# Reordering the prologue of a fused adaLN, attention and SwiGLU kernel: score banks kept free, dummy matmuls, statistics and normalisations on other engines

## The chip, the cores and the metric

The kernel runs on one core of one Trainium2 chip. The metric is the device time of one execution in microseconds (us), lower is better. The kernel before takes 1299.07 us (median of 4 runs, 1298.13 to 1301.06).

Engines in the profile: PE is TensorE's matmuls and PEld its weight loads, DVE is VectorE, ACT is ScalarE, POOL is GpSimd, SP is the engine that issues the loads.

## The reference

One transformer block with modulation (adaLN): 2048 tokens, width 1024, 32 heads of 32 that share one K and one V head, a SwiGLU of width 3584. All inputs are bf16.

```python
mod = (silu(c) @ w_mod).reshape(1, 6, 1, -1)          # w_mod: 1024 x 6144
sa, ca, ga, sb, cb, gb = ...                           # its six parts
h = layernorm(x) * (1 + ca) + sa
q = h @ wq; k = h @ wk; v = h @ wv                     # 32 query heads, one K, one V
p = softmax(q @ k.T * 32 ** -0.5)
x = x + ga * ((p @ v) @ wo)
h = layernorm(x) * (1 + cb) + sb
x = x + gb * ((silu(h @ w1) * (h @ w3)) @ w2)
```

Only the prologue matters here: loading x and the modulation weights, the first layernorm, K, V and the first Q, until the exponentials of the scores flow on ScalarE.

## The kernel before

The kernel file contains its own list scheduler. Each instruction is a node with an engine, what it reads and writes, a priority and an *assumed* duration `dur`. `schedule()` plays the engines forward with these durations and fixes the order of the instructions on every engine; `emit()` writes each engine's stream in that order with semaphore waits. On the chip each engine then works through its stream in that order.

```python
G.add("pe", tr, reads=[("XN", q0 + i), "IDENT"] + xnk(q0 + i), dur=ncb * 0.065, ...)   # one node
...
    t_free[e] = s + d                     # schedule(): the engine is free after the assumed duration
...
# loads, in this order: x tiles 0-7, modulation weights, K, V, first slice of Q
xload(0, 8)
for k in range(NC):
    dma(... WM01[:, k, :], wmod_in[k * P:(k + 1) * P, 0:2 * D] ..., ("wm01", k), writes=[("UR", k)], ...)
dma(... WKV[:, 0], wk_in ...); dma(... WKV[:, 1], wv_in ...); dma(... WQ[:, :, 0:P] ...)
...
# modulation columns (128 matmuls of one column, in 8 packs, one for each load), then two copies on VectorE
for k in range(NC):
    G.add("pe", mm, reads=["SCT", ("UR", k)], dur=16 * 0.06, ...)
G.add("dve", ... MODC[:, 0, :] ...); G.add("dve", ... MODC[:, 1, :] ...)
...
def ln_norm(t, q):                        # (x - mean) * rstd, 128x1024, on VectorE
    G.add("dve", lambda e: e.tensor_scalar(xnt(q), X[:, s, :], MV[:, t, 0:1], RS[:, t:t + 1],
                                           ALU.subtract, ALU.mult), ..., dur=0.42, prio=2)
...
for tb in range(NTB):                     # four blocks of 512 tokens = 4 tiles each
    for i in range(4):
        ln_stats(tb * 4 + i)              # 2 statistics halves and an aggregate on VectorE
    ln_scale(tb * 4, 4)                   # rstd of 4 tiles, two small GpSimd instructions
    for i in range(4):
        ln_norm(tb * 4 + i, q0 + i)
    if tb + 2 < NTB:
        xl = xload(tb * 4 + 8, 4)
    ln_transpose(4, q0, ..., ("act", "dve") if tb < 2 else ("dve",))   # PE transposes, HREG evictions with MODC
    kv(tb)                                # K and V of this block
    if tb == 0:
        qproj(0, 0)
```

A step of attention needs the keys of two tiles; the first head group therefore takes 4 exponentials of 128x1024 from each block of tokens, and the 13th exponential is the first that needs the fourth block's keys. The eight PSUM banks are two general ones (PB) and six (SP) that become score banks with the first score.

Three words used below: an eviction is the copy of PE's results from a PSUM bank into a buffer; the HREG evictions write the normalised tokens, transposed and modulated, from which K, V and Q are projected; the modulation columns (MODC) are the scale and shift that these evictions apply. Row scales are the layernorm's rstd.

The softmax here doesn't subtract the row's maximum and nothing guards it: scores larger than these inputs give would overflow.

## Time and profile before

| | before |
|---|---|
| time, median | 1299.07 us |
| ScalarE busy | 1011.0 us, 78% of the span; 1024 exponentials are 969.6 us of it |
| modulation columns read by VectorE | 21.09 us |
| first exponential | 38.05 us |
| 13th exponential | 61.86 us |

The first part of the page (busy time of each engine, its share of the span, number of instructions):

```profile
span 1296.0 us, 26693 instructions
PE 1177.5 (91%) x11393; PEld 583.5 (45%) x11393; DVE 877.7 (68%) x1223; ACT 1011.0 (78%) x1174; POOL 20.8 (2%) x51
```

The timeline of ScalarE (start, duration, engine, line, operation, what is written from what, shapes, count, and in brackets the idle time before and what ended it). L509 are HREG evictions, L715 the exponentials:

```profile
21.36 2.79 ACT L509 ACTIVATE HREG<-SP,MODC 128x512 bf16<-128x512 bf16 x4 [18.93 <-DVE MODC L457]
...
38.05 1.94 ACT L715 ACTIVATE UREG<-SP 128x1024 bf16<-128x1024 f32 x2 [3.78 <-PE SP L704]
43.87 5.61 ACT L715 ACTIVATE UREG<-SP 128x1024 bf16<-128x1024 f32 x6 [3.88 <-PE SP L704]
51.62 3.77 ACT L715 ACTIVATE UREG<-SP 128x1024 bf16<-128x1024 f32 x4 [2.15 <-PE SP L704]
61.86 3.77 ACT L715 ACTIVATE UREG<-SP 128x1024 bf16<-128x1024 f32 x4 [6.47 <-PE SP L704]
66.23 22.36 ACT L715 ACTIVATE UREG<-SP 128x1024 bf16<-128x1024 f32 x24 [0.60 <-PE SP L704]
```

Read it as a count: 2 + 6 + 4 exponentials, then the 13th at 61.86 us. Before that ScalarE waits; after it the exponentials run almost without a gap. So the place where the prologue pays or loses is the 13th exponential.

What leads there, from the timelines of the other engines: the last pack of modulation matmuls (L450) waits for its load, the columns are read at 21.09 us, and the four K projections (L538, 8 matmuls each) follow.

```profile
20.47 0.58 PE L450 MATMUL PB<-SCT,UREG 128*128 128x1 bf16 x16 [0.92 <-DMA UREG<-in_w_mod_dram]
20.73 1.04 POOL L459 COPY WKR<-QT 128x1024 bf16<-128x1024 bf16 x1 [2.69 <-DMA QT<-in_A_wk_dram]
21.09 0.17 DVE L455 COPY MODC<-PB 128x8 f32<-128x8 f32 x1 [1.10 <-PE PB L450]
24.20 3.59 PE L538 MATMUL SP<-HREG,WKR 128*128 128x512 bf16 x8 [3.15 <-ACT HREG L509]
37.87 3.59 PE L538 MATMUL SP<-HREG,WKR 128*128 128x512 bf16 x8
47.56 1.90 PE L538 MATMUL PB<-HREG,WKR 128*128 128x512 bf16 x8 [0.38 <-DVE HREG L515]
58.66 1.90 PE L538 MATMUL PB<-HREG,WKR 128*128 128x512 bf16 x8 [2.32 <-DVE HREG L515]
```

The first two projections take 3.59 us and the last two 1.90 us for the same work: PE's clock is at half in the first two. The Trainium skill, "TensorE: Matmul & The Clock Gate" (Part 1), describes this: half the clock until about 3.4 us of sustained work. The trace agrees in the ratio (3.59 / 1.90 = 1.9). The granted clock in the profile reads 0.5 around the second projection (36.6 to 43.4 us) but 1.00 around the first (24.2 to 27.8 us), so for the first the half clock is read from the durations alone.

### The profile page before, as it was taken

To read this page: it belongs to the slowest core of one execution; us is meant where nothing else is said; L and a number is where in the kernel's file an instruction comes from. 1 tells how busy PE (TensorE), PEld (TensorE's weight loads), DVE (VectorE), ACT (ScalarE), POOL (GpSimd) and SP (SyncE) were. 2 spreads that over 40 slices of the span, in tenths; PEclk is the share of its full clock that TensorE was granted. 3 is DMA by queue.
4 is the path that set the end of the run, shared out by engine and by line. 5 is a ranking of instruction groups with operands and counts; after the bars stand their busy time and mean duration, and the time that the engine had idled before them with its cause. 6 is when DMAs were issued, how large, how long until landed. Compare 5 with 4: busy or idle time off the path is not lost.

```text
span 1296.0 us, 26693 instructions
## 1 busy us (share of the span) xinstructions
PE 1177.5 (91%) x11393; PEld 583.5 (45%) x11393; DVE 877.7 (68%) x1223; ACT 1011.0 (78%) x1174; POOL 20.8 (2%) x51
## 2 busy tenths in 40 slices
PE   5698998899898889868999999999999999999998
PEld 3343344554455555413333335545333336754477
DVE  7888867885457787746687777656887777633421
ACT  1499999999899999989999999989999996011100
POOL 1000000000000000000000000000000000000000
PEclk9898999999899999868999999999999999999999
DMA  9533001553456556500232344202433244255563
GB/s 313 195 103 112 2 2 50 148 155 107 114 133 176 144 151 181 145 1 2 66 89 84 90 121 112 62 1 67 130 98 94 83 109 115 60 174 150 161 173 90
DMA packets 239446, 141.31 MB, mean 109 GB/s; under 512 B 6880, under 2 KB 231136, under 8 KB 239328
## 3 DMA queue, kind: packets, MB, share of 16 engines
q1 hardware_dynamic: 239328, 139.61, 37.6%
q8 instruction: 90, 1.47, 0.5%
q14 instruction: 28, 0.23, 0.1%
HBM read 135.40 MB, written 4.19 MB: 108 GB/s over the span
## 4 chain that ended last, share of the span: by engine, by line
PE 43%; ACT 41%; issue 6%; DVE 6%; DMA 3%; SPq 1%; ACTq 0%; DVEq 0%
ACT UREG L715 38%; PE PB L809 9%; PE PB L838 7%; PE SP L704 5%; PE SP L809 5%; PE PB L659 5%; PE SP L838 5%; ACT HREG L818 3%; PE PB L786 2%; DMA WREG<-in_B_w_dram 1%; DVE UREG L744 1%; PE PB L554 1%; PE PB L760 1%; DMA WREG<-in_w_mod_dram 1%; DMA UREG<-in_w_mod_dram 1%
## 5 line engine op out<-in xcount | busy, mean ns | idle before, releaser
L715 ACT ACTIVATE UREG<-SP 128x1024 bf16<-128x1024 f32 x1024 | 969.6, 1172 | 60.6 <-PE PB L659 32.1
L809 PE MATMUL PB<-QT,WREG 128*128 128x512 bf16 (+1 forms) x1904 | 361.7, 331 | 6.8 <-DVE DSB L766 2.0
L749 DVE TENSOR_TENSOR UREG<-UREG 128x2048 bf16<-128x2048 bf16 x200 | 243.2, 1216 | 31.8 <-ACT UREG L715 29.2
L704 PE MATMUL SP<-QT,KT 32*128 32x512 bf16 (+1 forms) x2560 | 207.5, 348 | 57.8 <-ACT UREG L715 44.2
L809 PEld LDWEIGHTS PB<-QT,WREG 128*128 128x128 bf16 x1904 | 166.8, 98 | 160.7 <-issue 63.3
L744 DVE TENSOR_TENSOR UREG<-UREG 128x2048 bf16<-128x2048 bf16 x100 | 121.5, 1215 | 87.3 <-ACT UREG L715 86.7
L704 PEld LDWEIGHTS SP<-QT,KT 32*128 32x128 bf16 x2560 | 54.1, 92 | 245.4 <-ACT UREG L715 231.0
L838 PE MATMUL PB<-WREG,HREG 128*128 128x256 bf16 x1232 | 152.8, 273 | 2.7 <-DVE HREG L843 1.8
L659 PE MATMUL PB<-UREG,V 128*32 128x512 bf16 (+1 forms) x2528 | 138.1, 353 | 10.2 <-DVE HREG L820 4.6
L838 PEld LDWEIGHTS PB<-WREG,HREG 128*128 128x128 bf16 x1232 | 113.1, 98 | 40.3 <-issue 24.8
L818 ACT ACTIVATE HREG<-PB 128x512 bf16<-128x512 f32 (+1 forms) x126 | 82.2, 652 | 46.9 <-PE PB L809 42.7
L769 DVE RECIPROCAL DSB<-DSB 128x128 f32<-128x128 f32 x128 | 115.1, 927 | 0.5
L820 DVE SCALAR_TENSOR_TENSOR HREG<-HREG,PB 128x512 bf16<-128x512 bf16 (+1 forms) x126 | 71.0, 563 | 45.8 <-ACT HREG L818 37.7
L659 PEld LDWEIGHTS PB<-UREG,V 128*32 128x32 bf16 x2528 | 59.2, 99 | 69.9 <-issue 25.8
L818 ACT ACTIVATE HREG<-SP 128x512 bf16<-128x512 f32 x14 | 8.4, 597 | 94.5 <-PE SP L809 94.5
L809 PE MATMUL SP<-QT,WREG 128*128 128x512 bf16 x336 | 75.0, 379 | 0.0
L554 PE MATMUL PB<-HREG,WREG 128*128 128x512 bf16 x256 | 66.2, 384 | 1.2 <-DVE QT L557 1.1
L825 DVE TENSOR_TENSOR HREG<-HREG,PB 128x256 bf16<-128x256 bf16 (+1 forms) x112 | 60.8, 543 | 5.4 <-PE PB L809 3.9
L838 PE MATMUL SP<-WREG,HREG 128*128 128x256 bf16 x560 | 62.8, 273 | 1.3 <-DMA WREG<-in_B_w_dram 1.3
L838 PEld LDWEIGHTS SP<-WREG,HREG 128*128 128x128 bf16 x560 | 54.6, 98 | 8.8 <-DMA WREG<-in_B_w_dram 1.8
L786 PE MATMUL PB<-WO,QT 128*128 128x512 bf16 x208 | 54.7, 390 | 0.1
L809 PEld LDWEIGHTS SP<-QT,WREG 128*128 128x128 bf16 x336 | 32.9, 98 | 39.4
(88 smaller groups left out, 567.0 us busy)
## 6 DMA issues: line engine op xcount, KB each, us to landing
WREG<-in_B_w_dram SPq DMA_DIRECT2D x140, 512.0 KB, 4.1
WREG<-in_B_w_dram SPq DMA_DIRECT2D x20, 1792.0 KB, 8.2
X<-in_A_x_dram SPq DMA_DIRECT2D x32, 256.0 KB, 3.7
WREG<-in_w_mod_dram SPq DMA_DIRECT2D x16, 512.0 KB, 4.9
UREG<-in_w_mod_dram SPq DMA_DIRECT2D x8, 512.0 KB, 9.1
out_dram<-X SPq DMA_DIRECT2D x16, 256.0 KB, 3.4
WO<-in_A_wo_dram SPq DMA_DIRECT2D x1, 2048.0 KB, 16.0
WREG<-in_A_wq_dram SPq DMA_DIRECT2D x1, 1792.0 KB, 11.1
```

What stands on the lines that cost most here:

```text
L554: g = mm_group(NC, lambda e, b, c: e.matmul(b, WQ[:, c, f * P:(f + 1) * P], HT[:, c, sl], start=c == 0, stop=c == NC - 1), lambda c: [("WQ ...
L659: r = e.matmul(PB[g.bank][32 * gg:32 * gg + 32, 0:qn], V[:, kt, :] if kind == "V" else ONES[:], U[:, pu, (gg * npk + j) * qn:(gg * npk + j ...
L704: r = e.matmul(SP[:, b, o:o + w], KT[32 * gg:32 * gg + 32, kts[j] * P:(kts[j] + 1) * P], QT[32 * gg:32 * gg + 32, f, q0 + qo:q0 + qo + w], ...
L715: G.add("act", lambda e, u=u, h0=h0, n=n, b0=b0, nb=nb, wb=wb: e.activation(U[:, u, h0 * W:(h0 + n) * W].rearrange("p (b w) -> p b w", b=n ...
L744: G.add("dve", lambda e, tr=tr, u=u, fu=first_u: e.tensor_tensor(TR[:, tr, 0:4 * W], U[:, fu, 0:4 * W], U[:, u, 0:4 * W], ALU.add), reads= ...
L749: G.add("dve", lambda e, tr=tr, u=u: e.tensor_tensor(TR[:, tr, 0:4 * W], TR[:, tr, 0:4 * W], U[:, u, 0:4 * W], ALU.add), reads=[("TR", tr) ...
L769: G.add("dve", lambda e, h=h: e.reciprocal(DSB[:, h * 128:(h + 1) * 128], DSB[:, h * 128:(h + 1) * 128]), reads=["DSB"], writes=[("DSBr", ...
L786: g = mm_group(NC, lambda e, b, f, t=t, h=h: e.matmul(b, QT[:, f, t * P:(t + 1) * P], WO[:, f, h * 512:(h + 1) * 512], start=f == 0, stop= ...
L809: return e.matmul(b[:, o:o + qn], W13[sl][w][:, c, sub * P:(sub + 1) * P], QT[:, c, q0:q0 + qn], start=c == 0, stop=c == NC - 1)
L818: G.add("act", lambda e, g=g1: e.activation(TS[:, 0:qn], PB[g.bank][:, 0:qn], ACT.Tanh, scale=0.5), writes=["TS"] + alias("TS"), groups=[( ...
L820: G.add("dve", lambda e, g=g1: e.scalar_tensor_tensor(TT[:, 0:qn], TS[:, 0:qn], 1.0, PB[g.bank][:, 0:qn], ALU.add, ALU.mult), reads=["TS"] ...
L838: return e.matmul(b[:, j * 256:(j + 1) * 256], HHT[:, fc, (i0 + j) * P:(i0 + j + 1) * P], W2S[:, r, fc, :], start=fc == 0, stop=fc == NF - 1)
```

## The change

Its intent: get two blocks of tokens ready before the first score, let no other work take a score bank once scores flow, and so start the exponentials earlier and without interruption; keep PE's clock up with dummy matmuls during the first loads; take statistics and a quarter of the normalisations off VectorE. The cut below leaves out smaller parts: the scheduler drops dummies that are not yet placed when the score banks close, counts 72 columns instead of 128 for a matmul of V, lets the first block's K and Q projections begin when their first chunk is there, and moves forward VectorE's long-waiting work only where its priority is low.

```diff
-    def __init__(self):                         # class Group
+    def __init__(self, lend=False):
...
-                if b in closed:                 # free_banks(): score banks only for groups that were lent one
+                if b in closed or (uses_left.get(b) and not grp.lend):
...
+    dma(... WKV[:, 0], wk_in ...)               # small K and V weights now first
+    dma(... WKV[:, 1], wv_in ...)
     xload(0, 8)
...
+    wm01(0, 2)
+    for i in range(120):                        # dummy matmuls, lowest priority
+        G.add("pe", lambda e, g=g: e.matmul(PB[g.bank][:, 0:P], IDENT[:], IDENT[:], start=True, stop=True),
+              reads=["IDENT"], dur=0.056, lat=0.2, acq=g if i == 0 else None, groups=[(g, "n")], mode="F", cls="W")
...
+    def ln_stats_act(t0, n):                    # sum and sum of squares of 4 tiles: 8 ScalarE passes
+        ... e.activation(xnt(t), X[:, s, :], ACT.Identity, accum_out=SUM[:, 0, t:t + 1]) ... dur=1.05
+        ... e.activation(xnt(t), X[:, s, :], ACT.Square, bias=SUM[:, 0, t:t + 1], accum_out=...) ... dur=1.05
...
-    def ln_norm(t, q):
-        G.add("dve", ...
-              ..., dur=0.42, prio=2)
+    def ln_norm(t, q, en="dve"):
+        G.add(en, ...
+              ..., dur=0.42 if en == "dve" else 1.2, prio=2)
...
+    def ln_front(tb):
+        if tb == 1:
+            ln_stats_act(4, 4)
+        else: ...
+        ln_scale(tb * 4, 4)
+        for i in range(4):
+            ln_norm(tb * 4 + i, tb * 4 % 12 + i, "pool" if i == 3 else "dve")   # every fourth on GpSimd
...
     for tb in range(NTB):
...
-        kv(tb)
-        if tb == 0:
+        if tb == 1:                             # K of two blocks and Q before the first score
+            kproj(0)
             qproj(0, 0)
+            lend[0] = False                     # from here on no score bank for other work
+            kproj(1); vproj(0); vproj(1)
+        elif tb:
+            kproj(tb); vproj(tb)
```

More of the change, by code (lines that the diff above doesn't have):

```diff
@@ L20 @@
 class Group:
-    def __init__(self):
+    def __init__(self, lend=False):
         self.bank = None
         self.nodes = []
+        self.lend = lend
 class Dag:
@@ L126, in bank_idle, with free_banks @@
             return None
-        def free_banks():
+        def free_banks(grp):
             out = []
             for b in banks:
-                if b in closed:
+                if b in closed or (uses_left.get(b) and not grp.lend):
                     continue
@@ L145, in schedule @@
                 tf = t_free[e]
-                fb = free_banks() if e == "pe" else None
+                if closed and e == "pe":
+                    drop = [n for n in ready[e] if n.cls == "W"]
+                    left -= len(drop)
+                    ready[e] = [n for n in ready[e] if n.cls != "W"]
+                    if not ready[e]:
+                        continue
+                fbs = {}
                 cands = []
@@ L151, in schedule @@
                     if n.acq is not None:
+                        k = n.acq.lend
+                        if k not in fbs:
+                            fbs[k] = free_banks(n.acq)
+                        fb = fbs[k]
                         if not fb:
@@ L178, in key @@
                         r = 0
+                    elif n.cls == "W":
+                        r = 9
                     elif n.cls is not None:
@@ L187, in key @@
                     p = n.prio
-                    if t - n.est > 4.0:
+                    if p > 2 and t - n.est > 4.0:
                         p -= 3
@@ L197, in schedule @@
             if n.acq is not None:
-                fb = free_banks()
+                fb = free_banks(n.acq)
                 b = fb[0][1]
@@ L366, in build @@
     RS = sb("RS", [P, NT], F32)
+    SUM = sb("SUM", [P, 2, NT], F32)
     NHALF = sb("NHALF", [P, 4], F32)
@@ L395, in build @@
     PBH = [p.bitcast(BF16) for p in PB]
+    lend = [True]
     def grp():
-        return Group()
+        return Group(lend[0])
     G.add("pool", lambda e: e.memset(ONES[:], 1.0), writes=["ONES"], dur=0.1)
@@ L418, in xload, with wm01 @@
         return r
-    xload(0, 8)
-    for k in range(NC):
-        dma(lambda e, k=k: e.dma_start(WM01[:, k, :], wmod_in[k * P:(k + 1) * P, 0:2 * D]), ("wm01", k),
-            writes=[("UR", k)], nbytes=P * 2 * D * 2)
+    WQK = [("WREG", "q")]
     dma(lambda e: e.dma_start(WKV[:, 0], wk_in.rearrange("(c p) f -> p c f", p=P)), "wk", writes=WKK, nbytes=65536)
     dma(lambda e: e.dma_start(WKV[:, 1], wv_in.rearrange("(c p) f -> p c f", p=P)), "wv", writes=WVK, nbytes=65536)
-    WQK = [("WREG", "q")]
-    dma(lambda e: e.dma_start(WQ[:, :, 0:P], wq_in[:, 0:P].rearrange("(c p) f -> p c f", p=P)), "wq0",
-        writes=[("WQ", 0)] + WQK, nbytes=P * D * 2)
+    xload(0, 8)
+    def wm01(k0, k1):
+        for k in range(k0, k1):
+            dma(lambda e, k=k: e.dma_start(WM01[:, k, :], wmod_in[k * P:(k + 1) * P, 0:2 * D]), ("wm01", k),
+                writes=[("UR", k)], nbytes=P * 2 * D * 2)
+    wm01(0, 2)
+    g = grp()
+    for i in range(120):
+        G.add("pe", lambda e, g=g: e.matmul(PB[g.bank][:, 0:P], IDENT[:], IDENT[:], start=True, stop=True),
+              reads=["IDENT"], dur=0.056, lat=0.2, acq=g if i == 0 else None, groups=[(g, "n")], mode="F", cls="W")
     G.add("act", lambda e: e.activation(CT[:], CROW[:], ACT.Tanh, scale=0.5), reads=["CROW"], writes=["CT"], dur=0.25)
@@ L445, in build, with ln_stats @@
             writes=[("QT", a, S - 512 + b) for b in range(0, 512, P)], dur=0.6)
+    def ln_stats(t):
+        s, q = t % NXS, t % 4
+        for a in range(2):
+            G.add("dve", lambda e, a=a: e.bn_stats(ST[:, q, a, :], X[:, s, a * 512:(a + 1) * 512]), reads=[("X", s)],
+                  writes=[("ST", q, a)], dur=0.6, prio=2)
+        G.add("dve", lambda e: e.bn_aggr(MV[:, t, :], ST[:, q].rearrange("p a f -> p (a f)")),
+              reads=[("ST", q, 0), ("ST", q, 1)], writes=[("MV", t)], dur=0.15, prio=2)
@@ new lines, in ln_stats_act @@
+    def ln_stats_act(t0, n):
+        for i in range(n):
+            t, s = t0 + i, (t0 + i) % NXS
+            G.add("act", lambda e, t=t, s=s: e.activation(xnt(t), X[:, s, :], ACT.Identity, accum_out=SUM[:, 0, t:t + 1]),
+                  reads=[("X", s)], writes=[("XN", t), ("SUM", t)] + xnk(t), dur=1.05)
+        sk = [("SUM", t0 + i) for i in range(n)]
+        G.add("pool", lambda e: e.tensor_scalar(SUM[:, 0, t0:t0 + n], SUM[:, 0, t0:t0 + n], -1.0 / D, None, ALU.mult),
+              reads=sk, writes=sk, dur=0.3)
+        for i in range(n):
+            t, s = t0 + i, (t0 + i) % NXS
+            G.add("act", lambda e, t=t, s=s: e.activation(xnt(t), X[:, s, :], ACT.Square, bias=SUM[:, 0, t:t + 1],
+                                                          accum_out=SUM[:, 1, t:t + 1]),
+                  reads=[("X", s), ("SUM", t)], writes=[("XN", t), ("SQ", t)] + xnk(t), dur=1.05)
+        G.add("pool", lambda e: e.tensor_scalar(MV[:, t0:t0 + n, 0], SUM[:, 0, t0:t0 + n], -1.0, None, ALU.mult),
+              reads=sk, writes=[("MV", t0 + i) for i in range(n)], dur=0.3)
+        G.add("pool", lambda e: e.tensor_scalar(MV[:, t0:t0 + n, 1], SUM[:, 1, t0:t0 + n], 1.0 / D, None, ALU.mult),
+              reads=[("SQ", t0 + i) for i in range(n)] + [("MV", t0 + i) for i in range(n)],
+              writes=[("MV", t0 + i) for i in range(n)], dur=0.3)
@@ new lines, in ln_scale, with xnt @@
+    def ln_scale(t0, n):
+        rk = [("RS", t0 + i) for i in range(n)]
+        G.add("pool", lambda e: e.tensor_scalar(RS[:, t0:t0 + n], MV[:, t0:t0 + n, 1], EPS, None, ALU.add),
+              reads=[("MV", t0 + i) for i in range(n)], writes=rk, dur=0.3)
+        G.add("pool", lambda e: e.tensor_tensor(RS[:, t0:t0 + n], RS[:, t0:t0 + n], NHALF[:, 0:n], ALU.pow),
+              reads=rk + ["NHALF"], writes=rk, dur=0.4)
+    def xnt(q):
+        return XN[:, q, :] if q < 4 else UREG[:, (NU + NTR - 1) * 2048 - (q - 4) // 2 * 2048 + q % 2 * D:][:, 0:D]
@@ new lines, in xnk @@
+    def xnk(q):
+        return [] if q < 4 else [("UR", NU + NTR - 1 - (q - 4) // 2)]
+    def ln_norm(t, q, en="dve"):
+        s = t % NXS
+        G.add(en, lambda e: e.tensor_scalar(xnt(q), X[:, s, :], MV[:, t, 0:1], RS[:, t:t + 1],
+                                               ALU.subtract, ALU.mult),
+              reads=[("X", s), ("RS", t), ("MV", t)], writes=[("XN", q)] + xnk(q), dur=0.42 if en == "dve" else 1.2, prio=2)
+    def ln_front(tb):
+        if tb == 1:
+            ln_stats_act(4, 4)
+        else:
+            for i in range(4):
+                ln_stats(tb * 4 + i)
+        ln_scale(tb * 4, 4)
+        for i in range(4):
+            ln_norm(tb * 4 + i, tb * 4 % 12 + i, "pool" if i == 3 else "dve")
@@ new lines, in build @@
+    ln_front(0)
+    xload(8, 4)
+    wm01(2, NC)
+    dma(lambda e: e.dma_start(WQ[:, :, 0:P], wq_in[:, 0:P].rearrange("(c p) f -> p c f", p=P)), "wq0",
+        writes=[("WQ", 0)] + WQK, nbytes=P * D * 2)
+    ln_front(1)
+    xl = xload(12, 4)
+    dma(lambda e: e.dma_start(WQ[:, :, P:D], wq_in[:, P:D].rearrange("(c p) f -> p c f", p=P)), "wq1",
+        writes=[("WQ", 1)], nbytes=7 * P * D * 2, after=xl)
+    wo_load = dma(lambda e: e.dma_start(WO[:], wo_in.rearrange("(c p) f -> p c f", p=P)), "wo", writes=["WO"],
+                  nbytes=D * D * 2, after=xl)
@@ L446, in build @@
+    ln_front(2)
     g = grp()
@@ L460, in build @@
           writes=["WKR"], dur=1.3)
-    def ln_stats(t):
-        s, q = t % NXS, t % 4
-        for a in range(2):
-            G.add("dve", lambda e, a=a: e.bn_stats(ST[:, q, a, :], X[:, s, a * 512:(a + 1) * 512]), reads=[("X", s)],
-                  writes=[("ST", q, a)], dur=0.6, prio=2)
-        G.add("dve", lambda e: e.bn_aggr(MV[:, t, :], ST[:, q].rearrange("p a f -> p (a f)")),
-              reads=[("ST", q, 0), ("ST", q, 1)], writes=[("MV", t)], dur=0.15, prio=2)
-    def ln_scale(t0, n):
-        rk = [("RS", t0 + i) for i in range(n)]
-        G.add("pool", lambda e: e.tensor_scalar(RS[:, t0:t0 + n], MV[:, t0:t0 + n, 1], EPS, None, ALU.add),
-              reads=[("MV", t0 + i) for i in range(n)], writes=rk, dur=0.3)
-        G.add("pool", lambda e: e.tensor_tensor(RS[:, t0:t0 + n], RS[:, t0:t0 + n], NHALF[:, 0:n], ALU.pow),
-              reads=rk + ["NHALF"], writes=rk, dur=0.4)
-    def xnt(q):
-        return XN[:, q, :] if q < 4 else UREG[:, (NU + NTR - 2) * 2048 + (q - 4) * D:][:, 0:D]
-    def xnk(q):
-        return [] if q < 4 else [("UR", NU + NTR - 2 + (q - 4) // 2)]
-    def ln_norm(t, q):
-        s = t % NXS
-        G.add("dve", lambda e: e.tensor_scalar(xnt(q), X[:, s, :], MV[:, t, 0:1], RS[:, t:t + 1],
-                                               ALU.subtract, ALU.mult),
-              reads=[("X", s), ("RS", t), ("MV", t)], writes=[("XN", q)] + xnk(q), dur=0.42, prio=2)
     def ln_transpose(nt, q0, dst, dkeys, fs, fm, engs, prio=5):
@@ L533, in mm_group, with kproj, vproj @@
         return g
-    def kv(tb):
+    def kproj(tb):
         sl = slice(tb * 512, (tb + 1) * 512)
-        hk = lambda c: [("HT", c, tb), HKEY]
         g = mm_group(NC, lambda e, b, c: e.matmul(b, WKR[:, c].rearrange("p a f -> p (a f)"), HT[:, c, sl],
-                                                  start=c == 0, stop=c == NC - 1), lambda c: ["WKR"] + hk(c))
+                                                  start=c == 0, stop=c == NC - 1),
+                     lambda c: ["WKR", ("HT", c, tb), HKEY], late=0 if tb else NC - 1)
         G.add("dve", lambda e, g=g: e.tensor_copy(KT[:, sl], PB[g.bank]), writes=[("KT", tb)], groups=[(g, "r")],
               dur=dve_t(512), prio=1)
+    def vproj(tb):
         def vmm(e, b, i):
@@ L546, in vmm @@
                             WKV[:, 1, c, :], start=c == 0, stop=c == NC - 1)
-        g = mm_group(4 * NC, vmm, lambda i: WVK + hk(i % NC), n_cols=128, per=NC)
+        g = mm_group(4 * NC, vmm, lambda i: WVK + [("HT", i % NC, tb), HKEY], n_cols=72, per=NC)
         G.add("dve", lambda e, g=g: e.tensor_copy(V[:, tb * 4:tb * 4 + 4, :].rearrange("p t f -> p (t f)"),
@@ L555, in qproj @@
                                                   start=c == 0, stop=c == NC - 1),
-                     lambda c: [("WQ", min(f, 1)), ("HT", c, tb), HKEY] + WQK)
+                     lambda c: [("WQ", min(f, 1)), ("HT", c, tb), HKEY] + WQK, late=0 if tb or f else NC - 1)
         G.add("dve", lambda e, g=g: e.tensor_copy(QT[:, f, sl], PB[g.bank]),
@@ L563, in build @@
     for tb in range(NTB):
-        for i in range(4):
-            ln_stats(tb * 4 + i)
-        ln_scale(tb * 4, 4)
-        q0 = 4 if tb == 1 else 0
-        for i in range(4):
-            ln_norm(tb * 4 + i, q0 + i)
-        if tb + 2 < NTB:
-            xl = xload(tb * 4 + 8, 4)
-        ln_transpose(4, q0, lambda c, tb=tb: HT[:, c, tb * 512:(tb + 1) * 512],
+        if tb == 3:
+            ln_front(3)
+        ln_transpose(4, tb * 4 % 12, lambda c, tb=tb: HT[:, c, tb * 512:(tb + 1) * 512],
                      lambda c, tb=tb: [("HT", c, tb)], 0, 1, ("act", "dve") if tb < 2 else ("dve",))
-        kv(tb)
-        if tb == 0:
+        if tb == 1:
+            kproj(0)
             qproj(0, 0)
-    dma(lambda e: e.dma_start(WQ[:, :, P:D], wq_in[:, P:D].rearrange("(c p) f -> p c f", p=P)), "wq1",
-        writes=[("WQ", 1)], nbytes=7 * P * D * 2, after=xl)
-    wo_load = dma(lambda e: e.dma_start(WO[:], wo_in.rearrange("(c p) f -> p c f", p=P)), "wo", writes=["WO"],
-                  nbytes=D * D * 2, after=xl)
+            lend[0] = False
+            kproj(1)
+            vproj(0)
+            vproj(1)
+        elif tb:
+            kproj(tb)
+            vproj(tb)
     for f in range(1, NC):
```

## The prediction

> **What bounds the kernel now.** Of a span of 1296.0 us (the page) ScalarE is busy 1011.0, 969.6 of it with 1024 exponentials; the chain of waits: PE 43%, ScalarE 41%. The change touches only about the first 62 us. Timeline: the last modulation weights land at 20.46 us, the first HREG evictions start at 21.36; the first exponential starts at 38.05; the 13th starts at 61.86, after a ScalarE wait of 6.5 us, since it needs the keys of the fourth token block. Up to there VectorE is the limit: between 21.3 and 61.4 us it is busy about 36 us of 40 (groups by shape in that window: 16 statistics halves 10.0 us, 24 evictions 11.5, 8 normalisations 3.8, 4 sums of 2048 columns 4.8). Its waits there are mostly K projections, 2.9 + 2.0 us.
>
> **What the change does.**
> - Statistics of tiles 4-7 move to ScalarE (8 passes, estimate 1.0 us each from the 128x1024 exponentials' 0.94 us here). Before, VectorE did them between 8 and 17 us, while it had to wait for the modulation weights anyway. So this takes almost nothing off the chain.
> - Every fourth normalisation goes to GpSimd: after 21 us it takes 2 x 0.48 us off VectorE, but a GpSimd pass costs an estimated 1.1-1.5 us (its 128x1024 copy took 1.04 us).
> - The small K and V weights are loaded before x. Their 64-byte rows are slow: with the first Q slice (0.39 MB together) they took from 20.5 to about 23 us. The Trainium skill, "DMA: Bandwidth & Descriptors" (Specifications), puts line rate at 512 B and up; the trace agrees. Estimate: everything behind them, the modulation weights too, comes 1.5 us later: evictions at 22.9 us.
> - 120 dummy matmuls. The first K projection ran cold, 8 matmuls in 3.59 us, the second too; the third took 1.90. The Trainium skill, "TensorE: Matmul & The Clock Gate" (Part 1), has the half clock until about 3.4 us of sustained work; the trace agrees in ratio (3.59/1.90). The dummies should end by about 12 us; gaps until 23 us may make PE cold again. If not, up to 2.9 us of waits shrink.
> - Two blocks' evictions before the first score, banks then kept for scores: the first exponential moves from 38 to about 30-32 us. But the 9th and 13th still need the third and fourth blocks' keys, which still wait for VectorE.
>
> **Sum at the 13th exponential (estimate).** Start +1.5, normalisations -1.0, K waits -1 to -2, GpSimd's normalisations and the exposed waits for row scales +0.5: about 61.5 us against 61.86. The early exponentials run earlier and then wait. From there on PE and ScalarE have the same order in both builds, so the gain is that point's shift, -4 to +3 us.
>
> **Prediction.** 1298.5 us, 80% range 1293.0 to 1302.5. Chances: faster by over 2% 0.01, within 2% 0.985, slower 0.005.
>
> **What would show it.** First exponential at 29-33 us; then a ScalarE gap of about 10 us before the 9th (at 48-51) and about 8 us before the 13th (at 59-63). First evictions at 22-23.5. VectorE without long gaps until 58. K projections at about 1.9 us if the warm-up lasts. After 65 us both timelines the same but for a shift.
>
> **What would make it wrong.** The PE clock after the dummies, in the third block's wait (PE may idle from 34 to 38 us), or at 90-98 us, where the granted clock was 0.56 with PE waiting for gate weights; GpSimd's passes much longer beside VectorE; another delay of the loads than 1.5 us.

## The result, and the profile after

The changed kernel takes 1315.37 us (median of 4 runs, 1314.11 to 1316.20) against 1299.07 us: ratio 1.0123, 95% interval 1.0105 to 1.0140. Ratios here and below are the mean time of one kernel's fast runs over that of the other's fast runs of the same rounds, so they are not quite the ratio of the medians quoted. It is slower by 16.3 us, outside the predicted range of 1293.0 to 1302.5.

```profile
span 1312.3 us, 26854 instructions
PE 1178.0 (90%) x11422; PEld 595.0 (45%) x11513; DVE 872.2 (66%) x1207; ACT 1019.8 (78%) x1190; POOL 40.0 (3%) x58
```

The page hardly shows anything: GpSimd has doubled, to 3% of the span. The timeline of ScalarE shows where the time went (L574 evictions, L778 exponentials):

```profile
31.39 4.12 ACT L574 ACTIVATE HREG<-SP,MODC 128x512 bf16<-128x512 bf16 x6 [9.62 <-DVE MODC L550]
...
39.22 7.44 ACT L778 ACTIVATE UREG<-SP 128x1024 bf16<-128x1024 f32 x8 [2.37 <-PE SP L767]
62.49 3.77 ACT L778 ACTIVATE UREG<-SP 128x1024 bf16<-128x1024 f32 x4 [15.84 <-PE SP L767]
79.61 3.97 ACT L778 ACTIVATE UREG<-SP 128x1024 bf16<-128x1024 f32 x4 [13.34 <-PE SP L767]
84.17 22.14 ACT L778 ACTIVATE UREG<-SP 128x1024 bf16<-128x1024 f32 x24 [0.59 <-PE SP L767]
```

The first eight exponentials now run in one piece, as intended. But they start at 39.22 us, not earlier than before, then ScalarE waits 15.8 us and 13.3 us, and the 13th comes at 79.61 us instead of 61.86: 17.8 us later. From there on both kernels do the same: 4 exponentials, then 24 in 22 us. The loss is complete at the 13th exponential.

The other engines, from the same timeline. L512 are the normalisations, L543 the modulation matmuls, L565 the transposes, L602 the K projections:

```profile
12.28 2.18 DVE L512 TENSOR_SCALAR XN<-X,MV,RS 128x1024 bf16<-128x1024 bf16 x3 [1.49 <-POOL RS L500]
12.43 4.36 POOL L512 TENSOR_SCALAR XN<-X,MV,RS 128x1024 bf16<-128x1024 bf16 x1 [0.19 <-POOL RS L500]
...
23.61 1.46 DVE L512 TENSOR_SCALAR UREG<-X,MV,RS 128x1024 bf16<-128x1024 bf16 x3 [9.16 <-POOL RS L500]
24.82 3.91 POOL L512 TENSOR_SCALAR UREG<-X,MV,RS 128x1024 bf16<-128x1024 bf16 x1 [1.30 <-DVE UREG L512]
...
26.38 0.61 PE L543 MATMUL SP<-SCT,UREG 128*128 128x1 bf16 x16
28.79 0.61 PE L565 MATMUL SP<-IDENT,UREG 128*128 128x128 bf16 x4 [1.80 <-POOL UREG L512]
...
30.04 1.04 PE L543 MATMUL SP<-SCT,UREG 128*128 128x1 bf16 x32
31.12 0.17 DVE L548 COPY MODC<-SP 128x8 f32<-128x8 f32 x1 [6.05 <-PE SP L543]
...
47.21 5.05 POOL L512 TENSOR_SCALAR UREG<-X,MV,RS 128x1024 bf16<-128x1024 bf16 x1 [1.25 <-DVE UREG L512]
...
64.75 4.36 POOL L512 TENSOR_SCALAR XN<-X,MV,RS 128x1024 bf16<-128x1024 bf16 x1 [0.17 <-issue]
```

A GpSimd normalisation takes 3.91 to 5.05 us, where the scheduler assumed 1.2 and the prediction 1.1 to 1.5. VectorE needs 1.46 us for three. (The profiler's spans on GpSimd are rough, but this one holds: the pass from 24.82 us ends at 28.73, and the transposes that wait for it start at 28.79.) And PE's stream shows what that does: the last two packs of modulation matmuls (30.04 us, x32) stand behind transposes of the second block (28.79 us) that waited for GpSimd's pass. So the modulation columns come at 31.12 us instead of 21.09, although their weights were there long before (in g_both, below, where the last pack waits only for its load, it starts at 22.79 us).

The chain of waits just before the 13th exponential (start, duration, engine, tile, line) passes through the last GpSimd pass and then through a K projection at half clock:

```profile
64.75 4.37 POOL XN L512
...
69.60 1.90 DVE HREG L580 x4
71.50 1.13 DVE UREG L807
72.63 1.82 DVE HREG L580 x4
74.45 0.45 issue
74.90 3.19 PE PB L602 x7
```

### The profile page after: what moved, and what is told of

Its sections match the earlier page's. It is cut to its first block, busy times and chain, and to the rows that moved or that the text cites. A ratio compares the mean times of both kernels' runs of the same rounds, so it can differ in the third digit from the quotient of the medians.

```text
span 1312.3 us, 26854 instructions
## 1 busy us (share of the span) xinstructions
PE 1178.0 (90%) x11422; PEld 595.0 (45%) x11513; DVE 872.2 (66%) x1207; ACT 1019.8 (78%) x1190; POOL 40.0 (3%) x58
## 4 chain that ended last, share of the span: by engine, by line
ACT 41%; PE 40%; issue 6%; DVE 5%; DMA 2%; POOL 0%; ACTq 0%; SPq 0%; DVEq 0%
ACT UREG L778 38%; PE PB L872 9%; PE PB L901 7%; PE SP L872 5%; PE SP L767 5%; PE SP L901 5%; PE PB L722 5%; ACT HREG L881 3%; PE PB L849 2%; DVE UREG L807 1%; DMA WREG<-in_B_w_dram 1%; PE PB L823 1%; PE SP L849 1%; DMA WREG<-in_w_mod_dram 1%; DVE UREG L812 1%
## 5 line engine op out<-in xcount | busy, mean ns | idle before, releaser
L778 ACT ACTIVATE UREG<-SP 128x1024 bf16<-128x1024 f32 x1024 | 969.7, 1179 | 75.0 <-PE SP L767 42.3
L872 PE MATMUL PB<-QT,WREG 128*128 128x512 bf16 (+1 forms) x1861 | 354.5, 330 | 10.7 <-issue 4.2
L620 PE MATMUL PB<-HREG,WREG 128*128 128x512 bf16 x229 | 59.4, 382 | 3.7 <-issue 2.4
L849 PE MATMUL PB<-WO,QT 128*128 128x512 bf16 x191 | 50.7, 390 | 2.1 <-issue 1.6
```

The lines of the kernel that those rows point to most:

```text
L778: G.add("act", lambda e, u=u, h0=h0, n=n, b0=b0, nb=nb, wb=wb: e.activation(U[:, u, h0 * W:(h0 + n) * W].rearrange("p (b w) -> p b w", b=n ...
L849: g = mm_group(NC, lambda e, b, f, t=t, h=h: e.matmul(b, QT[:, f, t * P:(t + 1) * P], WO[:, f, h * 512:(h + 1) * 512], start=f == 0, stop= ...
L872: return e.matmul(b[:, o:o + qn], W13[sl][w][:, c, sub * P:(sub + 1) * P], QT[:, c, q0:q0 + qn], start=c == 0, stop=c == NC - 1)
```

## The experiments

The theories:

- **G**: the GpSimd normalisations cost the time, 4 us each in four blocks.
- **P**: the order in PE's queue costs it: ready modulation matmuls stand behind transposes that wait.
- **L**: the small K and V weights, loaded first, delay everything.
- **C**: the dummy matmuls upset PE's clock; or **W**: PE goes cold in the new waits.

All times below are medians. "Columns" is the moment VectorE reads the modulation columns, "13th" the start of the 13th exponential in the profile of that kernel.

| kernel | what it is | time us | ratio to before (95%) | columns us | 13th us |
|---|---|---|---|---|---|
| before | | 1299.07 | 1 | 21.09 | 61.86 |
| changed | | 1315.37 | 1.0123 (1.0105-1.0140) | 31.12 | 79.61 |
| a_dvenorm | changed, all normalisations on VectorE | 1305.40 | 1.0053 (1.0040-1.0066) | 25.68 | 69.08 |
| b_poolnorm | before, every fourth on GpSimd | 1300.32 | 1.0013 (0.9999-1.0027) | 22.09 | 63.81 |
| c_truedur | changed, scheduler told 4.4 us | 1303.70 | 1.0030 (1.0013-1.0047) | 27.19 | 68.81 |
| d_nodummy | a without dummy matmuls | 1305.13 | 1.0048 (1.0036-1.0061) | 25.98 | 68.87 |
| e_modfirst | a, modulation matmuls first | 1301.55 | 1.0022 (1.0011-1.0034) | 22.80 | 66.34 |
| f_warm | a, dummies before the 3rd and 4th K | 1303.75 | 1.0028 (1.0016-1.0040) | 26.36 | 67.71 |
| g_both | e and f | 1297.89 | 0.9991 (0.9979-1.0002) | 23.41 | 63.26 |
| h_load | g, K and V weights later | 1299.12 | 0.9996 (0.9984-1.0008) | 21.81 | 63.77 |
| k_pool | g, GpSimd normalisations back, 4.4 us told | 1303.59 | 1.0032 (1.0020-1.0044) | 25.39 | 65.24 |
| i_actev | g, half of the later evictions on ScalarE | 1298.38 | 0.9990 (0.9978-1.0003) | 22.80 | 61.07 |
| j_act3 | i, fourth block's statistics on ScalarE | 1296.97 | 0.9981 (0.9968-0.9993) | 23.02 | 60.78 |
| l_base | before, with i's evictions | 1307.44 | 1.0057 (1.0045-1.0069) | 21.11 | 70.67 |
| m_pool01 | changed, GpSimd only in blocks 1 and 2 | 1311.32 | 1.0089 (1.0073-1.0106) | 31.20 | 75.27 |
| n_pool23 | changed, GpSimd only in blocks 3 and 4 | 1313.93 | 1.0107 (1.0087-1.0128) | 26.09 | 75.96 |
| p_best | j, K and V weights later | 1296.68 | 0.9982 (0.9970-0.9995) | 22.18 | 59.31 |

(o_forms, below, has one run only.) The runs were made in three sessions on three chips: a to d, e to h, and i to p. The kernel before ran in each, with medians of 1298.88, 1299.12 and 1299.39 to 1299.53 us; where kernels of different sessions are compared, the ratios are safer than the medians.

Over all these kernels the 13th exponential moves from 59.3 to 79.6 us and the time from 1296.7 to 1315.4: what is lost or won there is nearly what is lost or won in all, to within about 3 us. One part of the remainder can be named. In the profiles of i_actev, j_act3 and k_pool the stretch after the last exponential is 2.6 to 3.2 us longer than in g_both: about 155 us into it PE waits 2.2 to 2.9 us for weights (1.39 us in g_both), and the granted clock is then at half for 3.4 us (1.00 in g_both). This has nothing to do with the prologue, and whether the runs that were not profiled have it is not known.

### a_dvenorm: normalisations back on VectorE

```diff
-            ln_norm(tb * 4 + i, tb * 4 % 12 + i, "pool" if i == 3 else "dve")
+            ln_norm(tb * 4 + i, tb * 4 % 12 + i, "dve")
```

> The changed kernel with all normalisations back on VectorE, nothing else undone. Theory G (the four GpSimd normalisations, about 4.4 us each where 1.2 was assumed, hold up PE's in-order stream and so the modulation and the later key projections): 15 to 18 us come back, 1296 to 1301 us, first HREG eviction at 22 to 24 us instead of 31.4, 13th exponential at about 60 to 63 us instead of 79.6. Theory L (the small K and V weights first, and the later start of loads, cost most): still 1308 us or more. Theory C (the dummy matmuls upset the PE clock): still 1308 us or more, granted clock near 0.7 in the first 140 us.

1305.40 us: 10.0 of the 16.3 us come back, but not all. Theory G names the largest part and is not the whole. The order is not what changed: `schedule()`, played off the chip, gives this kernel the same order as the changed one on ScalarE and in all but 12 of 5713 places on PE. The timeline shows two things that remain. First, PE's order: modulation matmuls (L543) again behind transposes (L565) of the second block, which wait for VectorE's normalisation (L512), this time because ScalarE's eight statistics passes and GpSimd's row scales end only at 20 us.

```profile
20.14 1.91 DVE L512 TENSOR_SCALAR UREG<-X,MV,RS 128x1024 bf16<-128x1024 bf16 x4 [5.69 <-POOL RS L500]
...
22.90 0.61 PE L543 MATMUL SP<-SCT,UREG 128*128 128x1 bf16 x16
23.38 1.44 PE L565 MATMUL PB<-IDENT,UREG 128*128 128x128 bf16 x12
24.61 1.04 PE L543 MATMUL SP<-SCT,UREG 128*128 128x1 bf16 x32
25.68 0.17 DVE L548 COPY MODC<-SP 128x8 f32<-128x8 f32 x1 [3.64 <-PE SP L543]
...
41.37 1.90 PE L722 MATMUL PB<-UREG,V 128*32 128x256 bf16 x32 [2.44 <-ACT UREG L778]
...
50.12 3.60 PE L602 MATMUL PB<-HREG,WKR 128*128 128x512 bf16 x8 [2.22 <-DVE HREG L580]
...
64.19 3.60 PE L602 MATMUL PB<-HREG,WKR 128*128 128x512 bf16 x8 [1.91 <-DVE HREG L580]
```

Second, the third and fourth K projections take 3.60 us each; in the kernel before they took 1.90. Both are taken up below.

### b_poolnorm: GpSimd's normalisations on the kernel before

```diff
-            ln_norm(tb * 4 + i, q0 + i)
+            ln_norm(tb * 4 + i, q0 + i, "pool" if i == 3 else "dve")      # dur 1.2, as in the change
```

> The kernel before with only this added: every fourth normalisation of the four prologue blocks on GpSimd. Theory G: slower by 8 to 17 us, 1307 to 1316 us, the GpSimd passes at 3.9 to 5 us each. Theories L and C: at most 3 us slower, since nothing of the loads and no dummy matmul is in it.

1300.32 us, ratio 1.0013: a miss for theory G as it stood. The passes are just as slow there (3.91 to 4.36 us), but little waits for them (the columns come 1.0 us later; of the 1.95 us at the 13th exponential, 1.7 are the fourth K projection, which ran at half clock here, 3.59 instead of 1.90 us): in the order of the kernel before, the modulation matmuls and the first block's K stand ahead of the second block's transposes, and the last two passes run while VectorE still has other work. A slow instruction costs only where something is queued behind it.

### c_truedur: the scheduler is told the truth

```diff
-              ..., dur=0.42 if en == "dve" else 1.2, prio=2)
+              ..., dur=0.42 if en == "dve" else 4.4, prio=2)
```

> The changed kernel, GpSimd passes kept, but the scheduler told that one takes 4.4 us instead of 1.2, so that it orders PE's stream around it. If the loss is mainly the wrong order (modulation matmuls queued behind transposes that wait for GpSimd): about half comes back, 1304 to 1309 us, the first HREG eviction at 22 to 25 us. If the pass itself is the loss in every block, whatever the order: 1311 to 1316 us.

1303.70 us: 11.7 of the 16.3 us come back with the GpSimd passes still there, only by another order. It is even level with a_dvenorm. So the 10.0 us above are the price of slow passes in an order that was made for fast ones, not of slow passes as such. What moved: only the last pack of modulation matmuls still waits (columns at 27.19 us), and VectorE does the fourth block's statistics earlier, so that GpSimd's last pass starts at 53.25 us instead of 64.75.

### d_nodummy: a_dvenorm without the 120 dummy matmuls

```diff
-    for i in range(120):
+    for i in range(0):
```

> As a_dvenorm, without the 120 dummy matmuls. If the dummies help: 1 to 3 us slower than a_dvenorm, the first K projection cold at about 3.5 us in both or only here. If they do nothing by the time of the first projection (the real work between leaves PE cold): within 1 us of a_dvenorm.

1305.13 against 1305.40 us: the dummies neither help nor harm, so theory C falls. In the changed kernel they do warm the clock (the last 83 of them take 4.81 us, 58 ns each), but by 15 us it is at half again, and the first K projection is cold with them (32.92 us here, 27.10 in a_dvenorm) and without (27.40 us in d_nodummy).

### e_modfirst, f_warm and g_both

e_modfirst adds one dependency, so that the second block's transposes stand behind all modulation matmuls. f_warm puts dummy matmuls where PE would wait before the third and fourth K projections. g_both has both.

```diff
# e_modfirst: in ln_transpose, for the second block only
-                reads=[("XN", q0 + i), "IDENT"] + xnk(q0 + i), ...
+                reads=[("XN", q0 + i), "IDENT"] + xnk(q0 + i) + [("MODC", 1)], ...
# f_warm: in attention, ahead of the first scores of the third and fourth block (steps 4 and 6)
+                for _ in range({4: 50, 6: 36}.get(i, 0)):
+                    G.add("pe", ... e.matmul(SP[:, b, 0:P], IDENT[:], IDENT[:], start=True, stop=True), reads=["IDENT"],
+                          writes=[("SP", b)], dur=0.1, lat=0.2, mode="F", cls="K")       # lowest priority
```

> a_dvenorm with one dependency added: the second block's transposes wait for the modulation columns, so that PE does all modulation matmuls first (in a_dvenorm the last three of eight stood behind transposes that waited until 21.6 us for the second block's normalisation). Theory P (order in PE's queue): modulation columns at 22 to 23.5 us instead of 25.7, 13th exponential 2 to 4 us earlier than 69.1, time 2 to 4 us below a_dvenorm (1305.4), 1301.5 to 1303.5. If the modulation is not on the chain: the same as a_dvenorm within 1 us.

> a_dvenorm with 50 and 36 dummy matmuls in PE's idle time before the third and fourth K projections (into score banks that are free then), which ran cold in 3.60 us each in a_dvenorm and in 1.90 us each in the kernel before. Theory W (PE goes cold in the waits that the change opened): both projections at 1.9 to 2.2 us, 13th exponential 2.5 to 3.5 us earlier, 1302 to 1303 us. If the cold clock is not on the chain: the same within 1 us; if the dummies get in the way: slower.

> Both of e_modfirst and f_warm. If the two losses add: 5 to 7 us below a_dvenorm, 1298.5 to 1300.5, level with the kernel before. If they overlap: no better than the better one of the two by 1 us.

e_modfirst: columns at 22.80 instead of 25.68 us and 1301.55 us, 3.9 us better. f_warm: 1303.75 us, 1.7 us better by the medians and about 3 by the ratios to before; the third projection was only partly warm (7 recorded matmuls in 2.43 us), so this one fell short of what was expected. g_both: 1297.89 us, 7.5 us better than a_dvenorm and level with the kernel before (0.9991). In g_both both projections are warm:

```profile
23.41 0.17 DVE L548 COPY MODC<-SP 128x8 f32<-128x8 f32 x1 [0.92 <-PE SP L543]
...
48.47 1.67 PE L602 MATMUL PB<-HREG,WKR 128*128 128x512 bf16 x7 [2.53 <-DVE HREG L580]
...
60.29 1.68 PE L602 MATMUL PB<-HREG,WKR 128*128 128x512 bf16 x7 [0.84 <-DVE HREG L580]
```

(One of the eight matmuls is shown apart or not recorded; 7 in 1.67 us is 0.24 us each, against 0.45 in a_dvenorm.) So with the normalisations on VectorE, the rest of the loss is two things: the order in PE's queue, and PE's clock in the waits that the new order opened. With both mended the change is worth nothing, but costs nothing.

### h_load: the small weights back behind the modulation weights

```diff
-    dma(... WKV[:, 0], wk_in ...); dma(... WKV[:, 1], wv_in ...)      # ahead of x
     ...
     wm01(2, NC)
+    dma(... WKV[:, 0], wk_in ...); dma(... WKV[:, 1], wv_in ...)
```

> g_both with the small K and V weights loaded after the modulation weights, as in the kernel before. Theory L (their 64-byte rows delay all later loads): modulation columns 1.5 to 2.5 us earlier than in g_both, 13th exponential 1 to 2.5 us earlier, 1 to 2.5 us faster than g_both. Rival: the K weights then come too late for the first K projection and it stays level within 1 us.

The columns do come 1.6 us earlier (21.81 against 23.41 us), but the 13th exponential does not (63.77 against 63.26), and the time is level (1299.12 us). The third K projection was cold again in the profiled run (7 matmuls in 3.13 us, 1.67 in g_both), which takes back about as much as the earlier columns gave. So theory L has the right size at the columns; in this chain no gain from it shows at the end, and how much there would be with a warm clock is not shown. The Trainium skill, "DMA: Bandwidth & Descriptors" (Specifications), puts line rate at 512 B and more for one transfer; these weights have rows of 64 B, and 128 KB in 1.6 us (80 GB/s, an estimate that takes the shift of the columns for the time of these loads; the stretch from 10 to 15 us of the changed kernel moved 409 GB/s) agrees.

### k_pool: the GpSimd passes once more, on g_both

```diff
-            ln_norm(tb * 4 + i, tb * 4 % 12 + i, "dve")                           # g_both
+            ln_norm(tb * 4 + i, tb * 4 % 12 + i, "pool" if i == 3 else "dve")     # dur=4.4
-                for _ in range({4: 50, 6: 36}.get(i, 0)):
+                for _ in range({4: 50, 6: 15}.get(i, 0)):
```

> g_both, but with every fourth normalisation on GpSimd again, and the scheduler told 4.4 us for each. Theory O (what cost time was the order that followed from a wrong duration, not the GpSimd passes themselves): within 1.5 us of g_both, 1297 to 1300 us. Theory G (the passes themselves cost): 1301 us or more.

1303.59 us: 5.7 us more than g_both, which is where theory G put it. But this does not make the passes the cause of all of it: at the 13th exponential k_pool is only 2.0 us behind g_both (65.24 against 63.26), and in the profiled runs 3.2 us are lost after the last exponential, at the wait described under the table, which i_actev has too without any pass on GpSimd. So theory O misses, by less than the time suggests. What the passes do can be seen: even with the right duration the pass occupies GpSimd, whose stream is in order: the first pass (13 to 17 us) stands ahead of the small instruction that ScalarE's second round of statistics needs, so the second block's row scales come later, VectorE's normalisations with them, and the modulation columns, which VectorE reads after those, at 25.39 us instead of 23.41. The clock was not mended after all: the third K projection was cold in this run (3.59 us). And 36 of the dummies ran from 42.35 to 46.33 us ahead of transposes; since these also need GpSimd's pass, which ended at 45.14, that is a delay of about 1 us. How the 2.0 us at the 13th exponential divide among these was not separated.

### m_pool01 and n_pool23: in which blocks the passes cost

```diff
-            ln_norm(tb * 4 + i, tb * 4 % 12 + i, "pool" if i == 3 else "dve")
+            ln_norm(tb * 4 + i, tb * 4 % 12 + i, "pool" if i == 3 and tb < 2 else "dve")     # m_pool01
+            ln_norm(tb * 4 + i, tb * 4 % 12 + i, "pool" if i == 3 and tb > 1 else "dve")     # n_pool23
```

> The changed kernel with GpSimd's normalisations only in the first two blocks; PE's order is that of the changed kernel. If the first blocks' passes cost the time (modulation columns at 31.1 us instead of 25.7): about 1311 us, 5 us or more above a_dvenorm (1305.4). If the last two blocks' do: within 2 us of a_dvenorm.

> The changed kernel with GpSimd's normalisations only in the last two blocks. Modulation columns back at about 25.7 us. If each block's pass costs its own delay: 4 to 6 us above a_dvenorm, 1309 to 1311 us, so that this and m_pool01 add up to the changed kernel (5.4 + 4.5, about 1315). If the last blocks' passes hide behind other waits: within 2 us of a_dvenorm.

m_pool01 keeps ScalarE's order of the changed kernel and PE's in all but 6 of 5713 places, and is 5.9 us above a_dvenorm; its columns come at 31.20 us, the same 5.5 us late as in the changed kernel. n_pool23 has the columns back (26.09 us) and is 8.5 us above a_dvenorm, with runs from 1309.4 to 1317.0. Both halves cost, each in its own place: the first two passes ahead of the modulation columns, the last two ahead of the third and fourth block's keys. By the medians the two add up to more than the 10.0 us of all four (5.9 + 8.5 = 14.4). By the ratios to before, which the different sessions call for, it is 4.7 + 7.0 = 11.7 us against 9.1, within the noise; so an overlap of the two is not shown.

### o_forms: why a pass takes 4 us

```diff
+            fn = [e.tensor_scalar(xnt(q), X[:, s, :], MV[:, t, 0:1], None, ALU.subtract),       # block 1
+                  e.tensor_scalar(xnt(q), X[:, s, :], 0.0, 1.0, ALU.subtract, ALU.mult),        # block 2
+                  e.tensor_scalar(xnt(q), X[:, s, :], 1.0, None, ALU.mult),                     # block 3
+                  e.tensor_copy(xnt(q), X[:, s, :])][t // 4]                                    # block 4
```

> The changed kernel with GpSimd's pass over 128x1024 in four forms, one in each block (the result is wrong on purpose): subtract with a per-partition column; subtract and multiply with constants; multiply with a constant; plain copy. If the number of arithmetic steps sets the time: about 2.4, 3.9, 2 and 1 us. If the per-partition column does: 3.9 us in the first and 1 to 1.5 us in the others. If any arithmetic form is slow and only the copy is fast: 3.5 us or more in the first three and 1 us in the copy.

The timeline of GpSimd, the four forms in that order:

```profile
12.91 3.13 POOL L514 TENSOR_SCALAR XN<-X,MV 128x1024 bf16<-128x1024 bf16 x1 [0.18 <-POOL RS L500]
24.05 3.77 POOL L515 TENSOR_SCALAR UREG<-X 128x1024 bf16<-128x1024 bf16 x1 [1.28 <-DVE UREG L512]
46.94 4.05 POOL L516 TENSOR_SCALAR UREG<-X 128x1024 bf16<-128x1024 bf16 x1 [1.23 <-DVE UREG L512]
64.12 1.04 POOL L517 COPY XN<-X 128x1024 bf16<-128x1024 bf16 x1
```

Any arithmetic form takes 3.1 to 4.1 us, with one step or two, with a column or with constants; only the copy takes 1.04 us. Each form ran once, beside different work of VectorE, so the differences among the three are not to be read. The prediction had taken the copy for the model of the normalisation. (The normalisation is wrong here for four tiles on purpose; the comparison with the reference passed all the same, so that comparison is not sensitive to it. One run, 1314.75 us, level with the changed kernel.)

### i_actev, j_act3, l_base and p_best: can the new order be made to pay

```diff
# i_actev = g_both and (40 and 30 dummies)            l_base = the kernel before and the same line
-                     ..., ("act", "dve") if tb < 2 else ("dve",))
+                     ..., ("act", "dve"))
# j_act3 = i_actev and
-        if tb == 1:
+        if tb in (1, 3):
             ln_stats_act(...)                          # assumed durations 1.25 instead of 1.05
# p_best = j_act3 and the K and V weights behind the modulation weights, as in h_load
```

> g_both with half of the HREG evictions of the third and fourth block on ScalarE, which waits there for scores anyway. Theory V (with order and clock mended, VectorE's work ahead of the third and fourth block's keys is the chain): 13th exponential 2 to 4 us earlier than g_both's 63.3, 1294 to 1296.5 us. If something else holds it: level with g_both (1297.9).

> i_actev with the fourth block's statistics on ScalarE too (8 passes of 1.25 us), 5.4 us less for VectorE before the fourth block's keys. Theory V: 13th exponential 1 to 4 us earlier than i_actev, 1291 to 1295 us. Rival: ScalarE's queue is in order, and the added passes hold back the evictions behind them or the first exponentials: no better than i_actev, or worse.

> The kernel before with only the ScalarE evictions of i_actev. If the new order of the change (two blocks before the first score) is worth anything: i_actev is faster than this by over 1 us. If not, this gains as much, 1295 to 1298 us, and the rest of the change is not needed.

> j_act3 with the small K and V weights loaded after the modulation weights. If that start counts: modulation columns at about 21.5 us instead of 23.0, 13th exponential 1 to 1.5 us earlier than 60.8, 1295 to 1296 us. If the first keys' weights or the clock give it back, as in h_load: level with j_act3 (1297.0).

i_actev moves the 13th exponential by 2.2 us, to 61.07, as theory V had it, but not the time (1298.38 us): in the profiled run the 2.6 us after the last exponential (under the table) take it back. j_act3 misses theory V: its 13th exponential comes only 0.3 us earlier than i_actev's. It reaches 60.78 us and 1296.97 us, and p_best 59.31 us and 1296.68 us, level with each other. Their ratios to before, 0.9981 and 0.9982, have intervals below 1: about 2.4 us faster than the kernel before. That is the best version found, and it is small.

l_base is the warning: the same one-line change on the kernel before costs about 8 us (ratio 1.0057). There the evictions stand in ScalarE's stream behind six exponentials, and VectorE, PE and the next keys wait for them; the next K projection is then cold:

```profile
43.47 5.61 ACT L715 ACTIVATE UREG<-SP 128x1024 bf16<-128x1024 f32 x6 [0.32 <-PE SP L704]
48.91 2.16 ACT L509 ACTIVATE HREG<-PB,MODC 128x512 bf16<-128x512 bf16 x3
49.79 1.90 PE L659 MATMUL PB<-UREG,V 128*32 128x256 bf16 x32 [3.00 <-ACT HREG L509]
...
53.74 3.59 PE L538 MATMUL PB<-HREG,WKR 128*128 128x512 bf16 x8 [1.09 <-DVE HREG L515]
```

In i_actev they stand behind the eight early exponentials and well ahead of the ninth, and i_actev is 9 us faster than l_base. So the new order makes room for these evictions; but i_actev also has the dummies and the modulation matmuls first, and their share in the 9 us was not separated.

## Why the prediction was wrong

The step that failed is this one: "a GpSimd pass costs an estimated 1.1-1.5 us (its 128x1024 copy took 1.04 us)", which the sum entered, with the exposed waits for row scales, as "+0.5". A pass takes 3.91 to 5.05 us (the profile after), any arithmetic form of it takes 3 us or more (o_forms), and the four together cost 10.0 us of the 16.3 (a_dvenorm), in an order that had been fixed for passes of 1.2 us: told 4.4 us, the scheduler gets 11.7 us back with the passes kept (c_truedur). The prediction had named "GpSimd's passes much longer beside VectorE" among its risks, but the pass from 24.82 us takes 3.91 us although VectorE is idle beside it from 25.07 us on, so the company of VectorE is not the main reason.

A second step failed with it: the modulation columns were put 1.5 us later, at "evictions at 22.9 us", as if their loads alone decided. They came at 31.12 us and the evictions at 31.39, because the sum looked at loads and VectorE and not at what stands ahead in PE's queue. The order was there to read before the run, since `schedule()` fixes it. This is 5.5 us with GpSimd's passes (m_pool01), and another 2.9 us without them (25.68 to 22.80 us, e_modfirst).

Walked from the changed kernel to g_both, the loss at the 13th exponential divides as follows: GpSimd's passes 10.5 us (79.61 to 69.08), PE's order 2.7 us (to 66.34), PE's clock 3.1 us (to 63.26); 1.4 us to the kernel before remain. The parts depend on the order in which they are taken, as c_truedur and k_pool show.

Point by point:

- *The 13th exponential decides, and what follows is the same.* Right: 17.8 us later there, 16.3 us in the time.
- *The early exponentials run earlier and then wait.* Half right. They ran in one piece of eight and then waited, but not earlier: 39.2 us, not 29 to 33; the waits were 15.8 and 13.3 us, not about 10 and 8.
- *ScalarE's statistics take almost nothing off the chain.* Right in sign, and too kind: they also made the second block's normalisations later, and with them the modulation matmuls queued behind (a_dvenorm).
- *The small weights delay what is behind them by 1.5 us.* Right: x is there at 5.42 instead of 4.05 us, and the columns move by 1.6 us in h_load. It did not reach the time there, where a cold third projection took it back.
- *The dummies end by 12 us and PE may be cold again by 23 us.* Right: they end at 10.3 us, and leaving them out changes nothing (d_nodummy).
- *K waits -1 to -2 us.* Wrong in sign: the third and fourth projections went cold. Named among the risks, with the right place (PE idle before the third block).
- *Within 2%: 0.985.* Right, but on the slow side: 1.2%, clear of the noise.

What stays open: how k_pool's 2.0 us at the 13th exponential divide, how often the wait after the last exponential occurs, and how much activity PE needs to keep its clock; the dummies of f_warm, h_load and k_pool did not always keep it.

## What to carry to other kernels

Before moving an instruction to another engine, time that very form there, not a copy of the same shape; and enter the measured duration in whatever decides the order, since here a wrong one hurt less by itself (b_poolnorm) than by what got queued behind it. When a change delays a stage, look at each in-order stream for ready work that stands behind an instruction that waits; here one dependency moved it ahead (e_modfirst, 3.9 us). Opening a wait of some microseconds on PE can cost a second time, by the half clock of the matmuls that end it.

## What the Trainium skill lacked or had wrong

- "GPSIMD Engine Reference" (4.1 Engine selection) calls one-input elementwise work on GpSimd "roughly line-rate", and section 8 puts VectorE at about twice its speed. Here a one-input pass with arithmetic over 128x1024 bf16 took 3.13 to 5.05 us on GpSimd against 0.49 us on VectorE (three in 1.46 us), 6 to 10 times; only the copy, 1.04 us, is near the page.
- The same page (1. Specifications) names contention with VectorE for two-port modes and for two inputs. The trace agrees for the normalisations: three on VectorE take 1.46 us alone and 2.18 us beside a pass, and the pass 4.36 instead of 3.91 us. It does not always show it for two inputs: in c_truedur a two-input sum of 2048 columns (1.21 us, from 45.72 us) lies within a pass of 3.91 us (from 43.69 us), neither of them longer; in the changed kernel such a sum (1.22 us, from 47.37 us) lies within the pass of 5.05 us (from 47.21 us).
- "TensorE: Matmul & The Clock Gate" (Part 1) gives the rule of no idle gap over about 3.4 us. In a_dvenorm PE was cold at 41.37 us (32 matmuls in 1.90 us, in the kernel before 1.06 us) after a longest gap of 2.44 us, following some 4 us in which it was busy only in short pieces; that page names frequent short idle times as a second way to lose the clock, but what share of a stretch has to be busy is on no page.
- No page says outright that dummy matmuls long before the work are of no use, though the same page's idle rule points that way: in a_dvenorm 120 of them end at 10.9 us, the granted clock is at half from 13.2 us, and they had no effect on a projection at 27 us (1305.13 us without them against 1305.40 us).
